# Gated linear attention and a mixture of experts in one kernel: ScalarE issues the small loads, VectorE's two scans run a step ahead, and the routing groups end at other tiles

## The chip, the cores and the metric

The kernel runs on one core of a Trainium2 chip. A core has five engines, each with its own instruction stream that it works off in order: TensorE (PE in the profile; its weight loads are shown apart as PEld), VectorE (DVE), ScalarE (ACT), GpSimd (POOL) and SyncE (SP). They meet through semaphores. Transfers between HBM and the on-chip memory run on 16 DMA engines; an instruction on SP, ACT or POOL starts one. The metric is the device time of one execution in microseconds.

## What is computed

First an attention with a decaying state, for 4 batches, 8 heads, 768 positions and a head size of 48; then a top-1 mixture of 8 experts over the 3072 rows that come out.

```python
for t in range(S):
    state = alpha[:, :, t, :, None] * state + np.einsum('bhd,bhe->bhde', k[:, :, t], v[:, :, t])
    y[:, :, t] = np.einsum('bhd,bhde->bhe', q[:, :, t], state)
...
logits = x @ w_gate + modality_bias[modality_id]
e_idx = np.argmax(logits, axis=1)
...
for e in range(E):
    mask = e_idx == e
    h = np.maximum(x[mask] @ w1[e], 0.0)
    out[mask] = gate_w[mask, None] * (h @ w2[e])
```

The gate weight `gate_w` is the softmax probability of the chosen expert. `x` has 384 columns, an expert's hidden layer 1024.

## The kernel before, in words

**Attention.** The 3072 rows are 24 tiles of 128, six to a batch. A loop over steps s = 0 to 23 is written as a pipeline: step s starts tile s and finishes earlier ones. `decay_in(s)` turns alpha on PE (L249) and copies it to a buffer X (on ACT, L258; two X buffers). `decay` (L263) and `decay_back` (L274) are two scans on DVE that make the running products of alpha, G and F. `scale(s-1)` turns k and q on PE and multiplies them with G and F on DVE (`kh` L290, `qh` L293). `rows(s-3)` turns a finished tile back (L369) and stores it to a DRAM buffer `xd`. `natural(s-1)` turns `kh` back (L299), `state`, `scores` and `outputs` (L331, L311, L338) are the products of the attention, `update` (L356) carries the state on. `logits` and `logits_rows` (L381, L389, L391) give the expert logits of two tiles at a time. `guard` (L278, ACT) looks for values of alpha out of range. The turned tiles share a ring of three PSUM buffers called `tr`; `scores` and the small products of the routing share a ring of two called `sc`.

**Loads.** `load` (L133) issues on SP one DMA for each of alpha, k, q and v of a tile: 1024 pieces of 192 bytes. A ring of four buffers holds each of alpha, k and q, six hold v; tile names end in the buffer, so `nat_a2` is alpha of tiles 2, 6, 10 and so on. SP also loads the gate weights `wgp` in four small DMAs at step 1 (L155), the modality numbers `mi` and biases `mbb` at step 2 (L161, L162), and stores `xd` (L374).

**Routing.** `GROUPS` lists (after, t0, t1): once the logits of tile `after` are there, tiles t0 to t1 - 1 are routed by a flow of small DVE and PE instructions which is cut into pieces. `advance()` runs the next piece of each open flow, twice in a step. The pieces of a group are A (L449 to L454), B (L457 to L464) and C (L467 to L477). For the two group ends named in `EARLY`, further pieces pick the fullest expert: D (L539 to L546) counts, E (L548 to L564) finds its rows and starts the load of its weights, F (L571, L527 to L532) makes their indices, G gathers them. So the experts' part can start before the routing of all tiles is known. Behind the loop, the last pieces are written out by hand among the last attention products and the first hidden units of the first early expert (`first_unit`, L124). `route_end` (L591) turns the counts into the table of the remaining work.

**Experts.** Long stretches of matmuls (L1007 to L1009, L1026 to L1028), each factor split into a rounded part and a rest. Weights come by SP (L665, L667), rows and gates by POOL (L693, L699).

**Order and semaphores.** PE, DVE and ACT run in the order of the program text; SP's and POOL's order comes from a scheduler when the program is built. The builder gives the DMAs that SP and ACT issue eight completion semaphores, DMAHW0 to DMAHW7, in turn by its own schedule. An instruction that issues a DMA waits until the earlier DMA on the same semaphore has landed.

Of the kernel before, what the change touches and what calls it, by code (L numbers as in the profile page):

```python
# [41 lines left out]
U = T // P  # L42
NG = 2 * E

EARLY = (16, 18)
NA = len(EARLY)
NE = NA * TE // T
SU = N // T
# [7 lines left out]
AMIN = 1.0e-17  # L56
AFLOOR = 1.0e-30

GROUPS = ((5, 0, 6), (11, 6, 12), (15, 12, 16), (17, 16, 18), (21, 18, 22), (23, 22, 24))


@with_exitstack
def attention_moe(ctx: ExitStack, tc: tile.TileContext, q, k, v, alpha, mid, wg, mb, w1, w2, out):
# [81 lines left out]

    warm(7)
    wgp = ac.tile([P, 2, 2, 32], F32, name="wgp")
    pool.memset(wgp, 0.0)
    mi = ac.tile([NU, P, 2], I32, name="mi")
    mbb = ac.tile([P, NM, E], F32, name="mbb")  # L150

    def load_gate():
        for c in range(2):
            for g in range(2):
                sp.dma_start(  # L155
                    wgp[64 * c : 64 * c + D, g, :, :E],
                    wg.rearrange("(h c g d) e -> c g d h e", c=2, g=2, d=D)[c, g],
                )

    def load_modality():  # L160
        sp.dma_start(mi.rearrange("t p w -> t (p w)"), mid.bitcast(I32).rearrange("(t x) -> t x", t=NU))  # L161
        sp.dma_start(mbb, mb.unsqueeze(0).broadcast_to([P, NM, E]))  # L162


    DR = na.tile([P, SEGS], F32, name="DR")[:, : NP * SEG + 1]
    vec.memset(DR, 0.0)
    vec.memset(DR[:, SEG :: SEG], 1.0)
# [53 lines left out]
    def bias_table():  # L221
        mf = ac.tile([NU, P], F32, name="mf")
        vec.tensor_copy(mf, mi[:, :, 0])
        yield
        mp = ps.tile([P, NU], F32, name="kv")
        pe.transpose(mp, mf, ident[:NU, :NU])
        mt = ac.tile([P, NU], F32, name="mt")
        vec.tensor_copy(mt, mp)
        tmp = ac.tile([P, NU, E], F32, name="btt")
        for m in range(NM):  # L230
            sel = ac.tile([P, NU], F32, name=f"msel{m}")
            vec.tensor_scalar(sel, mt, float(m), None, op0=ALU.is_equal)
            vec.tensor_tensor(
                tmp if m else bt,
                sel.unsqueeze(2).broadcast_to([P, NU, E]),
                mbb[:, m].unsqueeze(1).broadcast_to([P, NU, E]),
                op=ALU.mult,
            )
            if m:
                vec.tensor_tensor(bt, bt, tmp, op=ALU.add)  # L240


    def seg(t, lo):
        return t.rearrange("p (a b) -> p a b", b=SEG)[:, :, lo : lo + P]

    def trans(i, n):
        p = ps.tile([P, NP, P], F32, name="tr", bufs=3)
        for j in range(NP):
            pe.transpose(  # L249
                p[:, j], nat[n, i % NB][:, 2 * j : 2 * j + 2].rearrange("p a b -> p (a b)"), ident  # L250
            )
        if i < 2 or (i == 2 and n == "a"):
            warm(1)
        return p

    def decay_in(i):
        pa = trans(i, "a")
        (act.copy if i else vec.tensor_copy)(seg(X[i % 2][:, 1:], 0), pa)  # L258
# [18 lines left out]
    def guard(i):  # L277
        act.activation(  # L278
            junk.rearrange("p (a b) -> p a b", b=D),
            nat["a", i % NB][:, :, :D].bitcast(U32),  # L280
            AF.Relu,
            bias=bhi,
            scale=1.0,
            accum_out=gacc[:, i : i + 1],
        )

    def scale(i):
        kh = sb.tile([P, NP, P], F32, name="kh")
        pk = trans(i, "k")
        vec.tensor_tensor(kh, pk, seg(st[i, "G"][:, 1:], 1), op=ALU.mult)  # L290
        qh = sb.tile([P, NP, P], F32, name="qh", bufs=3)
        pq = trans(i, "q")
        vec.tensor_tensor(qh, pq, seg(st[i, "F"], 1), op=ALU.mult)  # L293
        st[i, "k"], st[i, "q"] = kh, qh

    def natural(i):
        p = ps.tile([P, NP, P], F32, name="tr", bufs=3)
# [133 lines left out]
    def route_begin():  # L431
        vec.memset(ohs, 0.0)
# [5 lines left out]
    def route_flow(t0, t1):  # L438
        n = t1 - t0
        s = slice(t0, t1)  # L440
        sh = [P, n, E]

        def wide(a, m=E):
            return a[:, s].unsqueeze(2).broadcast_to([P, n, m])

        def over(a, m=E):
            return a.unsqueeze(1).broadcast_to([P, n, m])

        vec.tensor_tensor(L[:, s], L[:, s], bt[:, s], op=ALU.add)  # L449
        vec.tensor_reduce(mx[:, s], L[:, s], axis=AX.X, op=ALU.max)  # L450
        vec.tensor_tensor(ls[:, s], L[:, s], wide(mx), op=ALU.subtract)
        vec.scalar_tensor_tensor(eq[:, s], ls[:, s], 0.0, over(rev), op0=ALU.is_equal, op1=ALU.mult)
        vec.tensor_reduce(m2[:, s], eq[:, s], axis=AX.X, op=ALU.max)
        vec.tensor_tensor(oh[:, s], eq[:, s], wide(m2), op=ALU.is_equal)  # L454
        yield
        rp = ps.tile([P, n, E], F32, name="sc", bufs=2)
        pe.matmul(rp, tri, oh[:, s], start=True, stop=False)  # L457
        for t in range(t0, t1 - 1):
            m = t1 - 1 - t
            pe.matmul(  # L460
                rp[:, t + 1 - t0 :], ones, oh[:, t].unsqueeze(1).broadcast_to([P, m, E]), start=False, stop=False
            )
        pe.matmul(rp, ones, ohs.unsqueeze(1).broadcast_to(sh), start=False, stop=True)
        vec.tensor_tensor(rk[:, s], rp, oh[:, s], op=ALU.mult)  # L464
        yield
        with nc.allow_low_precision("whole numbers"):
            vec.tensor_reduce(r1[:, s], rk[:, s], axis=AX.X, op=ALU.add)  # L467
        if t1 == NU and n > 2:
            vec.tensor_reduce(hsum, oh[:, t0 : t1 - 1].rearrange("p t e -> p e t"), axis=AX.X, op=ALU.add)
            vec.tensor_tensor(ohs, ohs, hsum, op=ALU.add)  # L470
        elif t1 < NU:
            vec.tensor_reduce(hsum, oh[:, s].rearrange("p t e -> p e t"), axis=AX.X, op=ALU.add)
            vec.tensor_tensor(ohs, ohs, hsum, op=ALU.add)
        vec.tensor_scalar(hr[:, s], r1[:, s], 7, None, op0=ALU.arith_shift_right)
        vec.tensor_scalar(lo[:, s], r1[:, s], P - 1, None, op0=ALU.bitwise_and)
        vec.scalar_tensor_tensor(hi[:, s], m2[:, s], -float(NU), hr[:, s], op0=ALU.mult, op1=ALU.add)
        vec.tensor_tensor(OL[:, s], over(ioh, P), wide(lo, P), op=ALU.is_equal)  # L477
# [113 lines left out]
    def route_end(na):  # L591
# [3 lines left out]
        cnt = ps.tile([P, E], F32, name="kv")  # L595
        pe.matmul(cnt, ones, ohs, start=True, stop=False)
        pe.matmul(cnt, ones, left, start=False, stop=False)
        if na:
            pe.matmul(cnt, ones, oh[:, NU - 2], start=False, stop=False)
        pe.matmul(cnt, ones, oh[:, NU - 1], start=False, stop=True)  # L600
        vec.tensor_tensor(
            nj.rearrange("p e u j -> p e (u j)"),
            cnt.unsqueeze(2).broadcast_to([P, E, 2 * NJ]),
# [239 lines left out]
    def split2(w, j):  # L843
        return split("w2", WR[w][1][:, 2 * j : 2 * j + 2])

    route_begin()
    mctx = ExitStack()
    manual = {mybir.EngineType.PE, mybir.EngineType.DVE, mybir.EngineType.Activation}
    mctx.enter_context(tc.manual_schedule(engines=manual))
    for s in range(NU):  # L850
        if s > 0 and s + PF < NU:
            load(s + PF, "a")
        if s > 0 and s + PF - 1 < NU:
            load(s + PF - 1, "kqv")
        if s == 1:
            load_gate()
        if s == 2:
            load_modality()
        if s == 4:
            sp.dma_start(xd[MID : MID + 1], zr)  # L860
            sp.dma_start(gd[MID : MID + 1], zr[:, 0:1])
        if s != 1:
            decay_in(s)
        if live(s - 1):
            scale(s - 1)
        if s == 1:
            decay_in(s)
        if live(s - 3):
            rows(s - 3)
        if live(s - 4) and s % 2:  # L870
            logits_rows(s - 4)
        advance()
        if live(s - 1) and (s - 1) % NC < NC - 1:
            natural(s - 1)
        decay(s)
        if s < NU - 1:
            advance()
        if s % 2:
            groups(s - 4)
        decay_back(s)  # L880
        guard(s)
        if s == 5:
            start(bias_table())
            half_index()
        if live(s - 3) and (s - 3) % 2:
            logits(s - 3)
        if live(s - 2):
            state(s - 2)
        if live(s - 1):
            scores(s - 1)  # L890
        if live(s - 2):
            outputs(s - 2)
        if live(s - 1):
            update(s - 1)
# [7 lines left out]
    hpool["h"] = rctx.enter_context(tc.tile_pool(name="hp", bufs=8, side="right"))  # L902
    w2s, hs = {0: []}, {0: []}

    advance()
    early = flows.pop()
    logits(L0 - 2)
    state(L0 - 1)
    scores(L0)
    outputs(L0 - 1)  # L910
    logits_rows(L0 - 2)
    group = route_flow(GROUPS[-1][1] - 4, GROUPS[-1][1])
    next(group)
    next(early)
    state(L0)
    rows(L0 - 1)
    next(group)
    outputs(L0)
    for _ in group:
        pass  # L920
    next(early)
    first_inputs()
    logits(L0)
    rows(L0)
    logits_rows(L0)
    last = route_flow(GROUPS[-1][1], NU)
    next(last)
    flag = out_of_range()
    next(flag)
    first_unit(0)  # L930
    next(last)
    ends = route_end(NE)
    next(ends)
    first_unit(1)
    next(early)
    first_unit(2)
    next(ends)
# [315 lines left out]
```

## Time and profile before

| | us |
|---|---|
| median of 3 runs | 374.81 |
| lowest and highest | 373.77 and 374.91 |
| the profiled execution, own time | 375.57 |
| its span, first to last instruction | 373.6 |
| mean granted PE clock | 0.989 |
| DVE, ACT, POOL busy | 224.8, 189.0, 151.6 |

In the profile, times count from the start of the span. A row of the timeline has the start, the length, the engine, the line, the operation and the tiles (out<-in), how many instructions it merges, and in brackets the idle time before it and what ended it. "SPq" marks an instruction of SP's that issues a DMA; its length is the time that SP spent on it, not the transfer. The attention loop runs to about 141 us, its end and the routing to 164 us, the experts from there.

### The profile page before, as it was taken

Reading aid. Unit: us, or ns where it says so; the run is one execution under the profiler, and the core shown is the slowest. Engines: PE = TensorE matmul, PEld = TensorE weight load, DVE = VectorE, ACT = ScalarE, POOL = GpSimd, SP = SyncE. Lnnn points to the kernel's source line nnn. Section 1 sums busy time; section 2 is a strip of 40 time slices with the busy share of each in tenths; the row PEclk is TensorE's granted clock in tenths of the full one; section 3 lists DMA queues with packets and bytes.
Section 4 is the critical chain, followed back from the end, with each engine's and each line's share of the span. In section 5 each row is a group of like instructions: output and inputs, shape, how many; then the busy total and the mean of one; then the engine's idle time right before and its main releaser. Section 6 shows DMA issues by size and latency. Waiting matters only on the chain. (4 is left out here: it accounts for less than half of the span.)

```text
span 373.6 us, 9370 instructions
## 1 busy us (share of the span) xinstructions
PE 359.1 (96%) x3666; PEld 317.0 (85%) x3666; DVE 224.8 (60%) x455; ACT 189.0 (51%) x367; POOL 151.6 (41%) x218
## 2 busy tenths in 40 slices
PE   7998999999999899999999999999999999999992
PEld 4787788889888788799998898899889988978992
DVE  6886979878979977895746506531661455036400
ACT  2666677677678464446554425433551454154310
POOL 9945244534444345283146335412722372220021
PEclk9999999999999989999999999999999999999997
DMA  9989999999999994849756416431723374110011
GB/s 139 165 123 159 208 192 194 183 185 190 198 183 186 194 380 160 294 171 359 223 157 204 155 44 227 154 107 48 270 84 120 131 214 145 45 44 5 1 45 49
DMA packets 122846, 59.18 MB, mean 158 GB/s; under 512 B 102977, under 2 KB 114296, under 8 KB 122792
## 3 DMA queue, kind: packets, MB, share of 16 engines
q1 hardware_dynamic: 118824, 48.83, 58.5%
q0 software_dynamic: 3968, 9.65, 7.7%
q8 instruction: 31, 0.51, 0.6%
q14 instruction: 23, 0.19, 0.2%
HBM read 49.01 MB, written 9.50 MB: 157 GB/s over the span
## 5 line engine op out<-in xcount | busy, mean ns | idle before, releaser
L973 POOL DMA_INDIRECT out_dram<-os,odx x23 | 23.1, 1004 | 110.0 <-ACT os L1041 93.3
L1007 PE MATMUL sc<-w2H,hH 128*128 128x384 f32 x192 | 65.0, 338 | 0.0
L316 POOL TENSOR_SCALAR_AFFINE_SELECT scT<-scT 128x512 f32<-128x512 f32 x48 | 38.4, 822 | 65.3 <-ACT scT L315 65.3
L1009 PE MATMUL sc<-w2H,hL 128*128 128x384 f32 x192 | 64.2, 334 | 0.0
L1008 PE MATMUL sc<-w2L,hH 128*128 128x384 f32 x192 | 64.2, 334 | 0.0
L837 DVE TENSOR_TENSOR w1L<-w1r,w1H 128x768 fp32r<-128x768 f32 x24 | 22.0, 955 | 67.6 <-ACT w1H L835 67.6
L1026 PE MATMUL tr<-xH,w1H 128*128 128x512 f32 (+1 forms) x144 | 53.8, 374 | 0.0
L1028 PE MATMUL tr<-xH,w1L 128*128 128x512 f32 (+1 forms) x144 | 53.5, 372 | 0.0
L1027 PE MATMUL tr<-xL,w1H 128*128 128x512 f32 (+1 forms) x144 | 53.5, 371 | 0.0
L829 DVE SCALAR_TENSOR_TENSOR hL<-tr,hH 128x512 fp32r<-128x512 f32 x47 | 32.4, 689 | 31.5 <-ACT hH L827 31.3
L827 ACT ACTIVATE hH<-tr 128x512 fp32r<-128x512 f32 x47 | 28.1, 598 | 45.5 <-PE tr L1028 42.0
L1041 ACT ACTIVATE os<-sc,gg 128x384 f32<-128x384 f32 x23 | 13.4, 582 | 67.4 <-PE sc L1009 43.5
L1007 PEld LDWEIGHTS sc<-w2H,hH 128*128 128x128 f32 x192 | 36.1, 188 | 1.1 <-issue 1.0
L1008 PEld LDWEIGHTS sc<-w2L,hH 128*128 128x128 f32 x192 | 36.1, 188 | 0.0
L1009 PEld LDWEIGHTS sc<-w2H,hL 128*128 128x128 f32 x192 | 36.0, 188 | 0.0
L699 POOL DMA_INDIRECT gg<-gd,idx x25 | 26.6, 1063 | 21.9 <-DMA gd<-gs 14.9
L315 ACT COPY scT<-sc 128x512 f32<-128x512 f32 x48 | 25.8, 589 | 12.6 <-PE sc L311 12.6
L693 POOL DMA_INDIRECT xg<-xd,idx x25 | 27.0, 1081 | 11.7 <-issue 4.9
L274 DVE TENSOR_TENSOR_SCAN Fw<-X,DF 128x516 f32<-128x516 f32 x24 | 31.0, 1291 | 0.8
L1028 PEld LDWEIGHTS tr<-xH,w1L 128*128 128x128 f32 x144 | 27.1, 188 | 4.7
L1026 PEld LDWEIGHTS tr<-xH,w1H 128*128 128x128 f32 x144 | 27.1, 188 | 4.6
L1027 PEld LDWEIGHTS tr<-xL,w1H 128*128 128x128 f32 x144 | 27.1, 188 | 4.6
(245 smaller groups left out, 684.2 us busy)
## 6 DMA issues: line engine op xcount, KB each, us to landing
w1r<-in_moe_w_dram SPq DMA_DIRECT2D x16, 768.0 KB, 4.8
w2r<-in_moe_w_dram SPq DMA_DIRECT2D x16, 768.0 KB, 4.5
nat_a<-in_alpha_dram SPq DMA_DIRECT2D x24, 192.0 KB, 3.7
nat_k<-in_k_dram SPq DMA_DIRECT2D x24, 192.0 KB, 5.5
nat_q<-in_q_dram SPq DMA_DIRECT2D x24, 192.0 KB, 4.8
vt<-in_v_dram SPq DMA_DIRECT2D x24, 192.0 KB, 4.6
xd<-xs SPq DMA_DIRECT2D x24, 192.0 KB, 4.9
xg<-xd,idx POOLq DMA_INDIRECT x25, 5.4
```

Of the source, the lines that this page charges most:

```text
L274: vec.tensor_tensor_scan(Fw, x[:, :-1], d, 0.0, op0=ALU.mult, op1=ALU.add)
L316: pool.affine_select(s, s, [[0, NP], [1, P]], ALU.is_ge, 0.0, base=0, channel_multiplier=-1)
L693: pool.indirect_dma_start(xg[x][:, u], None, xd[0:rows], IOA(idx[:, c : c + 1], 0), bounds_check=rows - 1, oob_is_err=False)
L699: pool.indirect_dma_start(gg[x][:, u : u + 1], None, gd[0:rows], IOA(idx[:, c : c + 1], 0), bounds_check=rows - 1, oob_is_err=False)
L827: act.activation(hH, hp, AF.Relu)
L829: vec.scalar_tensor_tensor(hL, hp, 0.0, hH.bitcast(F32), op0=ALU.max, op1=ALU.subtract)
L1007: pe.matmul(op, hH[:, us] if f is None else hH[:, f, us], wH, start=first, stop=False)
L1008: pe.matmul(op, hH[:, us] if f is None else hH[:, f, us], wL, start=False, stop=False)
L1009: pe.matmul(op, hL[:, us] if f is None else hL[:, f, us], wH, start=False, stop=final)
L1026: pe.matmul(hp, wH[:, d, fs], XH[:, d, :n], start=(d == 0), stop=False)
L1027: pe.matmul(hp, wH[:, d, fs], XL[:, d, :n], start=False, stop=False)
L1028: pe.matmul(hp, wL[:, d, fs], XH[:, d, :n], start=False, stop=(d == ND - 1))
```

## The change

ScalarE issues the six small loads: the four of `wgp` before the loop, `mi` and `mbb` at the start of step 3. The clearing of `wgp` moves from POOL to DVE. From step 8 on, `decay_in`, `decay` and `guard` run for the tile after the current one; from step 12 on `decay_back` too (at steps 8 and 12 both tiles are done). At step 0 `kh` is made right behind the first scan. The groups end at 6, 12, 16, 20 and 24 tiles instead of 6, 12, 16, 18, 22 and 24, and the early choices stand after 16 and 20 tiles, not 16 and 18. Three short dummy matmuls (`warm`) fall away. The bias table uses a `sc` buffer instead of `kv` and is cut into more pieces.

```diff
-EARLY = (16, 18)
+EARLY = (16, 20)
...
-GROUPS = ((5, 0, 6), (11, 6, 12), (15, 12, 16), (17, 16, 18), (21, 18, 22), (23, 22, 24))
+GROUPS = ((5, 0, 6), (11, 6, 12), (15, 12, 16), (19, 16, 20), (23, 20, 24))
+T0 = GROUPS[-1][1]
+LEAD = (8, 12)
...
-    pool.memset(wgp, 0.0)
+    vec.memset(wgp, 0.0)
...
-    def load_gate():
-        for c in range(2):
-            for g in range(2):
-                sp.dma_start(
...
-    def load_modality():
-        sp.dma_start(mi.rearrange("t p w -> t (p w)"), mid.bitcast(I32).rearrange("(t x) -> t x", t=NU))
-        sp.dma_start(mbb, mb.unsqueeze(0).broadcast_to([P, NM, E]))
...
+    for c in range(2):
+        for g in range(2):
+            act.dma_start(
+                wgp[64 * c : 64 * c + D, g, :, :E],
...
-        mp = ps.tile([P, NU], F32, name="kv")
+        mp = ps.tile([P, NU], F32, name="sc", bufs=2)
...
-        if i < 2 or (i == 2 and n == "a"):
+        if i == 0 or (i == 1 and n == "a"):
             warm(1)
...
+    def lead(s, w):
+        return [i for i in ((s, s + 1) if s == LEAD[w] else (s + (s > LEAD[w]),)) if i < NU]
...
-        if s == 1:
-            load_gate()
-        if s == 2:
-            load_modality()
...
+        if s == 3:
+            act.dma_start(mi.rearrange("t p w -> t (p w)"), mid.bitcast(I32).rearrange("(t x) -> t x", t=NU))
+            act.dma_start(mbb, mb.unsqueeze(0).broadcast_to([P, NM, E]))
+        ins = lead(s, 0)
         if s != 1:
-            decay_in(s)
+            decay_in(ins[0]) if ins else None
...
-        decay(s)
+        steps = [(decay, i) for i in lead(s, 0)] + [(decay_back, i) for i in lead(s, 1)]
+        steps.sort(key=lambda x: x[1])
+        for f, i in steps[:1]:
+            f(i)
+        if s == 0:
+            scale_keys(s)
         if s < NU - 1:
             advance()
         if s % 2:
             groups(s - 4)
-        decay_back(s)
-        guard(s)
+        for f, i in steps[1:]:
+            f(i)
+        for i in ins:
+            guard(i)
...
-    advance()
-    early = flows.pop()
+    (early,) = flows
+    next(early)
     logits(L0 - 2)
+    next(early)
     state(L0 - 1)
     scores(L0)
+    next(early)
     outputs(L0 - 1)
     logits_rows(L0 - 2)
-    group = route_flow(GROUPS[-1][1] - 4, GROUPS[-1][1])
-    next(group)
     next(early)
...
     first_unit(0)
+    first_unit(1)
     next(last)
     ends = route_end(NE)
     next(ends)
-    first_unit(1)
     next(early)
```

The next rows are ACT's in the changed kernel from the end of step 2 into step 3; before, the row of S is followed by that of X. S belongs to the state, X to alpha of tile 3, and the brackets name the semaphores waited for.

```order
L347 COPY yt<-y 128x512 [waits PE_49]
L359 COPY S<-kv 128x192 [waits PE_49]
L862 DMA mi<-in_moe_modality_id_dram 24x256 [waits DMAHW0_49]
L863 DMA mbb<-in_moe_modality_bias_dram 128x16 [waits DMAHW1_49]
L254 COPY X_165<-tr 128x4x128 [waits DVE_49,PE_49]
L374 COPY xs<-tr 128x2x4x48 [waits PE_49]
```

The two small loads stand ahead of the copies of step 3, and each waits for a DMA semaphore. SP's rows in the changed kernel, from v of tile 3 on, show who else uses these two semaphores (in brackets the semaphore of each DMA; buffers k0, q0 hold tile 4, a1 tile 5, a2 tile 6, k2 and q2 tile 6; vt4 and vt5 are v of tiles 4 and 5).

```order
L135 DMA vt3_109<-in_v_dram 128x8x48 [waits DMAHW4_49]
L135 DMA nat_a1_85<-in_alpha_dram 128x8x48 [waits DMAHW5_49,PE_49,Activation_49]
L135 DMA nat_k0_81<-in_k_dram 128x8x48 [waits DMAHW6_49]
L135 DMA nat_q0_83<-in_q_dram 128x8x48 [waits DMAHW7_49]
L135 DMA vt4_111<-in_v_dram 128x8x48 [waits DMAHW0_49]
L135 DMA vt5_113<-in_v_dram 128x8x48 [waits DMAHW1_49]
L859 DMA xd_60<-zr_188 1x384 [waits DMAHW2_49,Pool_49]
L860 DMA gd_61<-zr_188 1x1 [waits DMAHW3_49]
L135 DMA nat_k1_87<-in_k_dram 128x8x48 [waits DMAHW4_49,PE_49]
L135 DMA nat_q1_89<-in_q_dram 128x8x48 [waits DMAHW5_49,PE_49]
L135 DMA nat_a2_91<-in_alpha_dram 128x8x48 [waits DMAHW6_49,Activation_49]
L135 DMA vt0_103<-in_v_dram 128x8x48 [waits DMAHW7_49,PE_49]
```

The DMA after these on SP (`nat_k2`) takes DMAHW2: numbers 0 and 1 are those of `mi` and `mbb`. So the wait of `mi` is for four landings on DMAHW0 (alpha of tile 0, the fourth `wgp`, v of tile 2, v of tile 4), that of `mbb` for four on DMAHW1 (k of tile 0, alpha of tiles 2 and 4, v of tile 5). Before, the four loads of `wgp` stood between vt3 and nat_a1, and `mi` and `mbb` between vt4 and vt5.

DVE's rows from the last of piece E at step 21 to `kh` of step 22, first before the change, then with it.

```order
L564 TENSOR_TENSOR OHE<-OHE,tok_207 128x32
L449 TENSOR_TENSOR L<-L,bt 128x16
L450 TENSOR_REDUCE mx<-L 128x2
L451 TENSOR_TENSOR ls<-L,mx 128x16
L452 SCALAR_TENSOR_TENSOR eq<-ls,rev 128x16
L453 TENSOR_REDUCE m_213<-eq 128x2
L454 TENSOR_TENSOR oh<-eq,m_213 128x16
L271 TENSOR_SCALAR amin<-G 128x4
L272 RECIPROCAL DF_163<-amin 128x4
L274 SCALAR_TENSOR_TENSOR Fw<-X_161,DF_163 128x516
L290 TENSOR_TENSOR kh<-tr,G 128x512
```

```order
L565 TENSOR_TENSOR OHE<-OHE,tok_211 128x32
L267 TENSOR_SCALAR amin<-G 128x4
L268 RECIPROCAL DF_163<-amin 128x4
L270 SCALAR_TENSOR_TENSOR Fw<-X_161,DF_163 128x516
L286 TENSOR_TENSOR kh<-tr,G 128x512
```

Piece A of the group that ended at 18 is gone from this place. PE's rows behind the loop in the changed kernel, from the last scores on; before, the two counts (L539, L541) stood in step 23, ahead of the scores of tile 22.

```order
L312 MATMUL sc<-qh,kh 64x128 x16
L540 LDWEIGHTS ones
L540 MATMUL sc<-ohs,ones 128x8
L542 LDWEIGHTS ones
L542 MATMUL sc<-left,ones 128x8
L339 MATMUL y<-scT,vt_111 64x128 x8
L390 MATMUL kv<-ident,lts 128x128 x2
L332 MATMUL y<-qh,T_173 64x128 x8
L370 MATMUL tr<-ident,yt 128x128 x4
L572 LDWEIGHTS OL
L572 MATMUL sc<-OHE,OL 128x2
```

Piece D of the second early choice has moved behind the last scores, and piece F (L572) behind `state` and `rows`.

More of the change, by code (lines that the diff above doesn't have):

```diff
@@ L147, in attention_moe @@
     wgp = ac.tile([P, 2, 2, 32], F32, name="wgp")
-    pool.memset(wgp, 0.0)
+    vec.memset(wgp, 0.0)
     mi = ac.tile([NU, P, 2], I32, name="mi")
     mbb = ac.tile([P, NM, E], F32, name="mbb")
-    def load_gate():
-        for c in range(2):
-            for g in range(2):
[L155 to L158, printed above, removed]
-    def load_modality():
-        sp.dma_start(mi.rearrange("t p w -> t (p w)"), mid.bitcast(I32).rearrange("(t x) -> t x", t=NU))
-        sp.dma_start(mbb, mb.unsqueeze(0).broadcast_to([P, NM, E]))
+    for c in range(2):
+        for g in range(2):
+            act.dma_start(
+                wgp[64 * c : 64 * c + D, g, :, :E],
+                wg.rearrange("(h c g d) e -> c g d h e", c=2, g=2, d=D)[c, g],
+            )
     DR = na.tile([P, SEGS], F32, name="DR")[:, : NP * SEG + 1]
@@ L230, in bias_table @@
         for m in range(NM):
+            yield
             sel = ac.tile([P, NU], F32, name=f"msel{m}")
@@ L285, in guard, with scale_keys @@
         )
-    def scale(i):
+    def scale_keys(i):
         kh = sb.tile([P, NP, P], F32, name="kh")
@@ L290, in scale @@
         vec.tensor_tensor(kh, pk, seg(st[i, "G"][:, 1:], 1), op=ALU.mult)
+        st[i, "k"] = kh
+    def scale(i):
+        if i:
+            scale_keys(i)
         qh = sb.tile([P, NP, P], F32, name="qh", bufs=3)
@@ L293, in scale @@
         vec.tensor_tensor(qh, pq, seg(st[i, "F"], 1), op=ALU.mult)
-        st[i, "k"], st[i, "q"] = kh, qh
+        st[i, "q"] = qh
     def natural(i):
@@ L467, in route_flow @@
             vec.tensor_reduce(r1[:, s], rk[:, s], axis=AX.X, op=ALU.add)
-        if t1 == NU and n > 2:
+        if t1 == NU and t0 < T0:
             vec.tensor_reduce(hsum, oh[:, t0 : t1 - 1].rearrange("p t e -> p e t"), axis=AX.X, op=ALU.add)
@@ L597, in route_end @@
         pe.matmul(cnt, ones, left, start=False, stop=False)
-        if na:
-            pe.matmul(cnt, ones, oh[:, NU - 2], start=False, stop=False)
-        pe.matmul(cnt, ones, oh[:, NU - 1], start=False, stop=True)
+        for t in range(T0 if na else NU - 1, NU):
+            pe.matmul(cnt, ones, oh[:, t], start=False, stop=(t == NU - 1))
         vec.tensor_tensor(
@@ L861, in attention_moe @@
             sp.dma_start(gd[MID : MID + 1], zr[:, 0:1])
+        if s == 3:
+            act.dma_start(mi.rearrange("t p w -> t (p w)"), mid.bitcast(I32).rearrange("(t x) -> t x", t=NU))
+            act.dma_start(mbb, mb.unsqueeze(0).broadcast_to([P, NM, E]))
+        ins = lead(s, 0)
         if s != 1:
-            decay_in(s)
+            decay_in(ins[0]) if ins else None
         if live(s - 1):
             scale(s - 1)
-        if s == 1:
-            decay_in(s)
+        for i in ins[s != 1 :]:
+            decay_in(i)
         if live(s - 3):
@@ L916, in attention_moe @@
     rows(L0 - 1)
-    next(group)
+    next(early)
     outputs(L0)
-    for _ in group:
-        pass
-    next(early)
     first_inputs()
@@ L924, in attention_moe @@
     rows(L0)
+    next(early)
     logits_rows(L0)
-    last = route_flow(GROUPS[-1][1], NU)
+    last = route_flow(T0, NU)
     next(last)
```

## The prediction

> **What bounds the kernel now.** I read the page's busy times first, then its slices for PE.
>
> ```profile
> PE 359.1 (96%) x3666; PEld 317.0 (85%) x3666; DVE 224.8 (60%) x455; ACT 189.0 (51%) x367; POOL 151.6 (41%) x218
> PE   7998999999999899999999999999999999999992
> ```
>
> PE is busy all along, so the kernel is as long as PE's work and its few holes: span 373.6 less 359.1 busy leaves 14.5 us, some at both ends. A change that takes no work from PE (this one takes three short dummies) can only close holes or open new ones. The timeline of PE by step shows three of them.
>
> ```profile
> 36.24 0.66 PE L249 MATMUL tr<-ident,nat_a 128*128 128x128 f32 x4 [1.78 <-DMA nat_a<-in_alpha_dram]
> 38.81 0.64 PE L381 MATMUL kv<-yt,wgp 128*32 128x256 f32 x8 [0.41 <-DVE mt L228]
> 129.84 0.87 PE L299 MATMUL tr<-ident,kh 128*128 128x128 f32 x4 [1.63 <-DVE kh L290]
> ```
>
> A window of 4 us shows what follows the third.
>
> ```profile
> 130.00:134.00 4.00, 4.00 (x60) 2.71 (x59) 3.79 (x20) 1.45 (x4) 2.24 (x2) 0.57 1.03 388
> ```
>
> In a window's row the third number from the end is the granted clock. In the 4 us behind the 1.63 us hole it is 0.57: 4 x 0.43 = 1.7 us of PE's work lost. That hole costs 3.3 us, not 1.6.
>
> **The first hole: the loads are late.** The order of SP's DMAs and PE's wait say why.
>
> ```profile
> 18.89 1.12 SPq L133 DMA_DIRECT2D vt<-in_v_dram  x1
> 20.11 3.58 SPq L155 DMA_DIRECT2D wgp<-in_moe_w_gate_dram  x4
> ...
> 24.85 0.73 SPq L133 DMA_DIRECT2D nat_q<-in_q_dram  x1
> ...
> 26.41 1.37 SPq L161 DMA_DIRECT2D mi<-in_moe_modality_id_dram  x1
> 27.82 0.36 SPq L162 DMA_DIRECT2D mbb<-n_moe_modality_bias_dram  x1
> 28.23 0.43 SPq L133 DMA_DIRECT2D vt<-in_v_dram  x1
> ...
> 31.27 1.07 SPq L133 DMA_DIRECT2D nat_a<-in_alpha_dram  x1
> ```
>
> ```profile
> 20.00:22.00 2.00, 2.00 (x59) 1.83 (x60) 1.90 (x4) 1.60 (x4) 0.04 (x1) 1.00 1.14 172
> 22.00:24.00 2.00, 2.00 (x36) 1.95 (x33) 0.81 (x1) 1.80 (x5) 1.75 (x3) 1.00 0.18 16
> ```
>
> While SP issues the four `wgp` loads the traffic falls from 172 to 16 GB/s, and alpha of tile 6, issued at 31.27, comes 1.78 us late. Without the six small loads SP has 3.58 + 1.37 + 0.36 = 5.3 us more ahead of it, so this hole closes: **-1.8 us**. The Trainium skill, "DMA: Bandwidth & Descriptors", section "Issuing engines are not separate DMA queues", says that DMAs from several engines share the same 16 DMA engines and that a second issuer saves only the sequencer's time, usually little. By it the hole would stay and the sum below be 1.8 us higher. The 16 GB/s row speaks against that here: the sequencer's time was what the stream lacked.
>
> The second hole is the bias table's `kv` buffer; it gets a `sc` buffer and later pieces: **-0.4 us**. The third comes from DVE, where piece A of the group 16 to 18 stands ahead of the second scan and so of `kh`.
>
> ```profile
> 125.71 0.65 DVE L449 TENSOR_TENSOR L<-L,bt 128x16 f32<-128x16 f32 x1
> 127.56 0.16 DVE L271 TENSOR_SCALAR amin<-G 128x4 f32<-128x4 f32 x1
> ```
>
> A takes 127.56 - 125.71 = 1.85 us there, more than the hole, and the change has none at this place. The hole and its slow clock go: **-3.3 us**.
>
> **What the change adds: a wait on ACT.** The load of `mi` waits for the fourth landing on DMAHW0. SP's and ACT's rows give the four: alpha of tile 0, the last `wgp`, v of tile 2, v of tile 4. The load of `mbb` waits in the same way for v of tile 5, the 22nd load of the stream. ACT works in order, so behind these two stand the copy of X for tile 3 and all that ACT does later. The timeline of ACT and PE shows when ACT gets there.
>
> ```profile
> 17.62 0.33 ACT L358 COPY S<-kv 128x192 f32<-128x192 f32 x1
> 18.17 0.59 ACT L258 COPY X<-tr 128x512 f32<-128x512 f32 x1 [0.22 <-PE tr L249]
> 18.84 0.62 PE L369 MATMUL tr<-ident,yt 128*128 128x128 f32 x4
> ```
>
> ACT is there at about 18 us, when SP is still issuing v of tile 3 (18.89). PE's L369 needs the `tr` buffer that X's copy frees, and DVE's scan of tile 3 needs X, so PE and DVE stop too. When does v of tile 5 land?
>
> ```profile
> 4.81 1.07 SPq L133 DMA_DIRECT2D nat_a<-in_alpha_dram  x1
> ...
> L133 SPq DMA_DIRECT2D vt<-in_v_dram x5: 428/1090/1142, 8.4 to 28.2; - x5
> ```
>
> The view of line L133 in that stretch also has their time to land.
>
> ```profile
> DMA to landing us min/median/max: 4.6/5.0/5.4
> ```
>
> From alpha of tile 2 at 4.81 to v of tile 3 at 18.89 lie 11 loads, (18.89 - 4.81) / 11 = 1.28 us each, and the loads of v from 8.4 to 28.2 us land 5.0 us after issue (4.6 to 5.4). The next five (alpha 5, k 4, q 4, v 4, v 5) go on at that pace: v of tile 5 is issued at 18.89 + 5 x 1.28 = 25.3 and lands at 30.3. `mi` is issued before that, `mbb` takes 0.36, so X's copy starts at about 30.7 and not at 18.17: **+12.5 us**. None of these five loads waits for ACT's or PE's later work, so nothing hides the wait and nothing prolongs it.
>
> Bounds: if the pace rose to the 0.73 us of q's load right behind `wgp` (24.85), and the landing took 4.6 us, X's copy would start at 18.89 + 5 x 0.73 + 4.6 + 0.4 = 27.5, +9.3; if v of tile 5 came no sooner than before (28.23 + 4.6 = 32.8) and the issue took the 1.37 us of `mi`, at 34.2, +16.0.
>
> **The clock after that stop.** The trace has two nearest cases. The 1.63 us hole cost 1.7 us. The start gives the other end: PE works from 1.26 us on, and a dummy product takes 0.63 us still at 6.36 and 0.38 at 7.46.
>
> ```profile
> 1.26 3.17 PE L144 MATMUL y<-still 128*128 128x512 bf16 x7 [1.26 <-DVE still L139]
> 6.36 0.63 PE L144 MATMUL y<-still 128*128 128x512 bf16 x1
> 7.46 0.38 PE L144 MATMUL y<-still 128*128 128x512 bf16 x1
> ```
>
> That is some 6 us at half speed, 3.1 us lost. A stop of 12 us is nearer to the start than to the hole: **+2.5 us** (1.7 to 3.1). The Trainium skill, "TensorE: Matmul & The Clock Gate", section "What's actually happening", has a gate that halves the clock after an idle window of about 3.4 us and opens it after a busy one; by it the loss is half of 3.4 to 6.8 us, the same range. The length of the slow stretch here agrees; that a hole of 1.63 us was enough does not.
>
> **The other parts.** Behind the loop PE gets three new waits. The rows of before that price them:
>
> ```profile
> 144.78 1.07 ACT L315 COPY scT<-sc 128x512 f32<-128x512 f32 x2 [1.14 <-PE sc L311]
> ...
> 143.01 0.15 DVE L548 TENSOR_REDUCE base<-rest 128x1 f32<-128x8 f32 x1
> 144.75 0.20 DVE L564 TENSOR_TENSOR OHE<-OHE,tok 128x36 f16<-128x36 f16 x1
> 153.61 0.17 DVE L464 TENSOR_TENSOR rk<-sc,oh 128x16 f32<-128x16 f32 x1
> 155.67 0.27 DVE L617 SCALAR_TENSOR_TENSOR diag<-ident,kc,dz 128x52 bf16<-128x52 f32 x1
> ```
>
> Piece D's count now stands right behind the last scores and shares their two buffers, so it waits for the first of ACT's two copies: half of 1.07 and the way there, some 0.8 us. F needs E's chain, 144.75 + 0.20 - 143.01 = 1.94 us, with `state` and `rows` (about 1 us) to cover it: 1.1 us with the hops. The table's first product needs 155.67 + 0.27 - 153.61 = 2.3 us of DVE with one hidden unit (1.4 us) ahead of it where two stood: 0.8 us. The sum is 2.7; about 0.7 us of small holes that PE has at these places now goes: **+2.0 us** (0 if DVE, which does no scan in step 23, is ahead by that much; 3 if none of the holes goes). The second expert's weights are asked for some 3 us later, but are used only at about 165 us, with 8 us between their landing and that now.
>
> The scans a step ahead put a scan of 1.2 us more into step 8 and both scans into step 12; DVE's steps have 1.5 us of slack beside PE's 5.5. **+0.5 us** (0 to 1.5). The earlier `kh` of step 0 and the dummies change only what comes before ACT's stop, which ends at a time that the loads set: nothing.
>
> **The sum**, against the profiled execution's own 375.57 us: -1.8 - 0.4 - 3.3 + 12.5 + 2.5 + 2.0 + 0.5 = +12.0, 387.6 us. The median of the runs lies 0.76 us below that execution, so **386.8 us**, 3.2% slower.
>
> **Rivals.**
>
> *ACT does not stop.* Then the useful parts are left: 374.81 - 5.5 + 2.0 + 0.5 = **371.8 us**, faster. It needs v of tile 5 to have landed when ACT gets there at 18 us, or the DMA to be queued without holding ACT. Against the first: 21 loads take 21 x 1.28 us at the trace's pace; the wait vanishes only from a pace under 0.6 us per load. Against the second: the table of SP's waits shows an issuer that stands at a wait, up to 6.9 us for ACT.
>
> ```profile
> SPq L374 <- ACT xs L373: 9.6, 4, 6.9
> ```
>
> Chance 0.10.
>
> *It does not stop, and the earlier alpha is late.* From step 8 on alpha is turned one step sooner. Before, alpha of tile 9 was issued here:
>
> ```profile
> 47.47 0.37 SPq L133 DMA_DIRECT2D nat_a<-in_alpha_dram  x1
> 47.57 0.66 PE L249 MATMUL tr<-ident,nat_a 128*128 128x128 f32 x4
> ```
>
> The page's list of DMA issues has the landing of alpha, from issue, in its last column.
>
> ```profile
> nat_a<-in_alpha_dram SPq DMA_DIRECT2D x24, 192.0 KB, 3.7
> ```
>
> With 3.7 us to land that is 51.2, and step 8 would want it at about 49: up to 2.2 us back, 374.0 us, no change. With ACT's stop the loads get far ahead and this is nothing. Chance 0.04.
>
> *ACT stops and more is lost.* The new holes behind the loop, 2.7 us within some 10, bring the clock to half once more, as the 1.63 us did: +1.7, 388.5 us. It lies within the range. Chance 0.15.
>
> **How the numbers follow.** ACT's stop has 0.86 in all, of which 0.71 for the sum and 0.15 with a second slow stretch. The bounds of its terms added at one end give 374.81 + 9.3 + 1.7 - 5.5 = 380.3 and at the other 374.81 + 16.0 + 3.1 - 5.5 + 3 + 1.5 = 392.9; 381 to 392 holds nearly all of the 0.86, say 0.8. A measurement of this kernel can tell about 0.3% (1.1 us) from no change. Faster than that: 0.10; within it: 0.04; slower: 0.86.
>
> **What would show it.** In the timeline of the changed kernel ACT's row of X for tile 3 would stand at about 31 us with an idle time of some 13 us ended by a DMA of v or by `mi`/`mbb`, PE's slices near the tenth of the span would be empty, and the granted clock behind them 0.5. PE's waits for alpha (1.8 us) and for `kh` (1.6 us) would be gone, and PE would wait at the count, at the product of OHE and OL and at the table's product behind the loop. If X's copy still starts near 18 us, the forecast is wrong and the first rival holds.

## The result: 3.5% slower

The changed kernel takes 388.46 us (median of 4 runs, 387.38 to 388.98), the kernel before 374.86 us (four runs now). The ratio is 1.035 (95% interval 1.030 to 1.040). The profiled execution of the changed kernel took 388.75 us, its span is 386.7 us, 13.1 us more than before's 373.6.

The page of the changed kernel, first PE's busy time, then its slices and the granted clock in the same 40 slices of 9.7 us:

```profile
PE 359.7 (93%) x3666; PEld 318.0 (82%) x3666; DVE 223.4 (58%) x442; ACT 189.3 (49%) x367; POOL 152.7 (39%) x217
...
PE   7807999999999999889999999999999999999992
...
PEclk9975999999999999999999999999999999999999
```

PE has the same work (359.7 against 359.1 us). Its third slice is empty and the fourth runs at about half clock: that is where the time went. The timeline of ACT, from the end of step 2 on, names the instructions:

```profile
17.48 0.33 ACT L359 COPY S<-kv 128x192 f32<-128x192 f32 x1
29.05 0.56 ACTq L862 DMA_DIRECT2D mi<-in_moe_modality_id_dram  x1
30.25 0.36 ACTq L863 DMA_DIRECT2D mbb<-n_moe_modality_bias_dram  x1
30.71 0.58 ACT L254 COPY X<-tr 128x512 f32<-128x512 f32 x1 [12.90 <-DMA vt<-in_v_dram]
```

ACT is done with S at 17.8 us and issues `mi` only at 29.05. SP's rows say what it waited for: the two loads of v of tiles 4 and 5, issued from 23.76 on in 2.31 us.

```profile
23.76 2.31 SPq L135 DMA_DIRECT2D vt<-in_v_dram  x2
```

The three loads just ahead of them (issued from 20.21 on) land 5.2 to 5.3 us after issue, so v of tile 4 is there at about 29.0, the time of `mi`, and v of tile 5, issued at 24.93, at about 30.1, the time of `mbb`. The copy of X, which could have run at about 18.0, starts at 30.71. PE, in its own timeline, stops with it:

```profile
18.26 0.60 PE L245 MATMUL tr<-ident,nat_q 128*128 128x128 f32 x4
31.35 1.11 PE L370 MATMUL tr<-ident,yt 128*128 128x128 f32 x4 [12.49 <-ACT X L254]
```

The windows of the same stretch show the clock (third number from the end):

```profile
18.90:23.30 4.40, 0.00 (x0) 0.00 (x0) 0.85 (x2) 0.00 (x0) 0.85 (x2) 1.00 1.07 174
23.40:31.30 7.90, 0.00 (x0) 0.00 (x0) 0.00 (x0) 0.58 (x1) 0.00 (x0) 0.50 1.38 164
31.40:37.00 5.60, 5.60 (x66) 4.94 (x68) 2.74 (x4) 2.48 (x6) 0.15 (x1) 0.50 1.24 187
37.00:41.00 4.00, 4.00 (x57) 3.20 (x53) 1.92 (x3) 2.63 (x6) 2.18 (x4) 1.00 0.54 104
```

The clock falls to half 4.5 us into the stop and stays there for the first 5.7 us in which PE works again: 2.8 us of work lost. The DMA engines move 164 to 174 GB/s all through the stop. The loads did not stop, only the compute engines did.

The table of PE's waits for the rest of the attention and the routing (total us, times, longest):

```profile
PE tr L300 <- DVE kh L286: 1.6, 3, 0.6
...
PE sc L540 <- ACT scT L316: 0.7, 1, 0.7
PE kv L682 <- DVE nj L601: 0.5, 1, 0.5
PE y L332 <- ACT yt L347: 0.5, 1, 0.5
PE kv L622 <- DVE diag L617: 0.4, 1, 0.4
PE tr L245 <- DMA nat_a<-in_alpha_dram: 0.4, 1, 0.4
PE kv L623 <- DVE diag L619: 0.2, 1, 0.2
```

The wait of 1.78 us for alpha of tile 6 is gone, and of that of 1.63 us for `kh` of tile 21 there is 0.58 us left (at 142.83, one of the three in the first row). The rows from L540 on, without the one for alpha, are new waits behind the loop.

### The profile page after: what moved, and what is told of

It is laid out like the page before. It is cut to its first block, busy times and chain, and to the rows that moved or that the text cites. A ratio compares the mean times of both kernels' runs of the same rounds, so it can differ in the third digit from the quotient of the medians.

```text
span 386.7 us, 9342 instructions
## 1 busy us (share of the span) xinstructions
PE 359.7 (93%) x3666; PEld 318.0 (82%) x3666; DVE 223.4 (58%) x442; ACT 189.3 (49%) x367; POOL 152.7 (39%) x217
## 5 line engine op out<-in xcount | busy, mean ns | idle before, releaser
L981 POOL DMA_INDIRECT out_dram<-os,odx x23 | 23.9, 1039 | 108.7 <-ACT os L1049 92.9
L259 DVE TENSOR_TENSOR_SCAN G<-X,DR 128x516 f32<-128x516 f32 x24 | 30.4, 1268 | 11.6 <-ACT X L254 11.6
L316 ACT COPY scT<-sc 128x512 f32<-128x512 f32 x48 | 25.8, 589 | 13.9 <-PE sc L312 13.9
```

Of the source, the lines that this page charges most:

```text
L259: vec.tensor_tensor_scan(G[:, 1:][:, ::-1], x[:, 1:][:, ::-1], DR[:, 1:][:, ::-1], 0.0, op0=ALU.mult, op1=ALU.add)
```

## The experiments

**e1: the two loads at step 1.** Theory: ACT's stop is a wait for landings that stand far ahead in the stream. Rivals: the two DMAs cost this time wherever ACT issues them, or something of step 3 does it. At step 1 the same two DMAs wait only for early `wgp` landings.

```diff
-        if s == 3:
+        if s == 1:
             act.dma_start(mi...)
             act.dma_start(mbb...)
```

> The changed kernel with the loads of mi and mbb issued by ACT at step 1, not 3. There each of the two waits for one landing of a small load of wgp (DMAHW2 and DMAHW4), which the changed kernel's trace has at 5.6 to 8 us, before ACT gets there at about 6.5 us or little later. Theory (the stop is the wait for landings far ahead in the stream of loads): no stop of more than 1.5 us, the stop of 12.5 us and the slow clock of 2.8 us behind it go, 388.5 - 15.3 = 373.2 us (372.2 to 374.5). Rival (the issue of these two DMAs on ACT among its copies, or their traffic, costs the time wherever it stands): 385 us or more.

Measured: 377.84 us, ratio to before 1.010 (1.007 to 1.014), span 375.8 us. ACT's copy of X of tile 3 starts at 18.03 us:

```profile
17.49 0.33 ACT L359 COPY S<-kv 128x192 f32<-128x192 f32 x1
18.03 0.59 ACT L254 COPY X<-tr 128x512 f32<-128x512 f32 x1 [0.22 <-PE tr L245]
```

The stop is gone, so its cause is the wait and not the DMAs. But 373.2 us was expected, and 4.6 us are missing. The timeline of PE and that of SP show where they are:

```profile
45.87 0.60 PE L245 MATMUL tr<-ident,nat_q 128*128 128x128 f32 x4
49.77 1.09 PE L245 MATMUL tr<-ident,nat_a 128*128 128x128 f32 x4 [3.30 <-DMA nat_a<-in_alpha_dram]
```

```profile
46.12 0.39 SPq L135 DMA_DIRECT2D nat_a<-in_alpha_dram  x1
```

```profile
49.20:52.50 3.30, 2.73 (x13) 2.43 (x13) 1.86 (x2) 1.06 (x2) 0.00 (x0) 0.50 1.29 194
```

At step 8, the first with the scans ahead, PE wants alpha of tile 9 at 46.5 us. SP issues its load at 46.12 and it lands at 49.63. The window behind it has half clock, 1.4 us lost. Together 4.7 us. In the changed kernel this hole does not show, because the stop let the loads run ahead: there alpha of tile 9 lands at 50.94 and is used at 61.49.

**e2: the two loads at step 2.** There they wait for the landings of q of tile 3 and alpha of tile 5.

```diff
-        if s == 3:
+        if s == 2:
```

> The changed kernel with the two loads on ACT at step 2. Now mi waits for the third landing on DMAHW3, that of q of tile 3, and mbb for the third on DMAHW5, that of alpha of tile 5, which the changed kernel's trace has at 20.21 + 5.22 = 25.4 us. Theory: ACT is there at 13.0 us and makes its copy of X of tile 2 at about 25.8, a stop of 12.8 us, one step earlier than in the changed kernel and ended by an alpha load, not a v load; half clock behind it for 3.4 to 6.8 us of work; 387 to 390 us. Rival (what stops ACT is something of step 3 alone, such as the buffers that X of tile 3 and v of tile 5 use): 373 us, no stop.

Measured: 388.13 us, ratio 1.037 (1.032 to 1.042). ACT's timeline:

```profile
12.37 0.34 ACT L359 COPY S<-kv 128x192 f32<-128x192 f32 x1
23.13 0.56 ACTq L862 DMA_DIRECT2D mi<-in_moe_modality_id_dram  x1
25.54 0.36 ACTq L863 DMA_DIRECT2D mbb<-n_moe_modality_bias_dram  x1
25.99 0.58 ACT L254 COPY X<-tr 128x512 f32<-128x512 f32 x1 [13.29 <-DMA mi<-in_moe_modality_id_dram]
```

X of tile 2 is copied at 25.99 (25.8 expected). The stop goes with the landings that the two DMAs wait for, one step earlier and at another copy; the rival of step 3 alone falls.

**e3: the two loads at step 3, issued by POOL,** whose DMAs do not use the eight semaphores.

```diff
         if s == 3:
-            act.dma_start(mi...)
-            act.dma_start(mbb...)
+            pool.dma_start(mi...)
+            pool.dma_start(mbb...)
```

> The changed kernel with the two loads at the same place, step 3, issued by POOL, whose DMAs don't use these eight semaphores. Theory: no wait, ACT's copy of X of tile 3 at about 18 us, 373.2 us (372.2 to 375, since POOL may be late with its own work by 1 to 2 us). Rival (the traffic of the two loads at that time, or a late mi, stops the pipeline): 385 us or more.

Measured: 379.05 us, ratio 1.013 (1.007 to 1.019). X of tile 3 is copied at 18.49: no stop at the same place in the program. POOL issued the two loads already at 5.38 and 6.13 us, so e3 takes them out of ACT's order but does not try their traffic at the time of step 3. As in e1, PE waits for alpha of tile 9 (3.4 us), which the expectation left out.

**e4: the kernel before, with `mi` and `mbb` alone moved to ACT at step 3.**

```diff
-        if s == 2:
-            load_modality()
+        if s == 3:
+            act.dma_start(mi...)
+            act.dma_start(mbb...)
```

> The kernel before with one edit: mi and mbb are issued by ACT at the start of step 3 and not by SP in step 2; wgp stays on SP. The two wait for the fourth landing on DMAHW0 and DMAHW1, here of v of tiles 4 and 5. v of tile 5 was issued at 28.23 with 1.7 us of the two loads ahead of it on SP, so at 26.5 now, and lands at 31.5. Theory: ACT, there at 17.9 us, copies X of tile 3 at about 31.9; stop +13.7, slow clock +2.8, the wait for alpha of tile 6 gone -1.8: +14.7, 389.5 us (387 to 392). Rival (the loss belongs to the other parts of the change together, such as the scans ahead or the wgp loads on ACT): within 2 us of 374.9.

Measured: 386.92 us, ratio 1.037 (1.032 to 1.043), just below the range expected. ACT's timeline:

```profile
30.86 0.37 ACTq L859 DMA_DIRECT2D mbb<-n_moe_modality_bias_dram  x1
31.33 0.58 ACT L258 COPY X<-tr 128x512 f32<-128x512 f32 x1 [13.39 <-DMA vt<-in_v_dram]
```

The copy starts at 31.33 (31.9 expected), and this one edit makes as much of a loss as the whole change. The rest of the change is then worth about nothing beside the stop. Of the 2.6 us that are missing to the 389.5 expected, 1.6 are the slow clock behind the wait for `kh` of tile 21, which this execution does not have: from the k turn of tile 21 to that of tile 22 it takes 8.19 us, before 9.74. e5 to e8 take the rest apart without the stop.

**e5: e1 without the scans ahead.**

```diff
-LEAD = (8, 12)
+LEAD = (NU, NU)
```

> The kernel of e1 (loads of mi and mbb at step 1) without the scans a step ahead (LEAD after the last step). What is open: e1 has no stop and is still 1% above before, and its trace has one new hole, PE waiting 3.30 us for alpha of tile 9 at step 8, with half clock behind it (some 1.2 us), and 0.8 us ahead of kh at step 13. Theory A (these belong to the scans ahead, which want alpha of tile 9 one step sooner than the stream of loads brings it): both go, 5.3 us less than e1, 0.4 to 0.6% below before, about 372.5 us where before is 374 to 375. Theory B (the loads on ACT or the new groups make the late alpha): the wait for alpha stays, within 1 us of e1 (377.8).

Measured: 376.76 us, where the kernel before took 377.41 us beside it, ratio 0.998 (0.995 to 1.001). Against e1's 1.010 that is 1.2%, 4.6 us: the wait for alpha of tile 9 is gone and so is the slow clock behind it. The scans ahead cause both (theory A). It is no clear gain over before, though; 0.4 to 0.6% was expected.

**e6: e5 with the groups, and the work behind the loop, of before.** It is before with `wgp` on ACT and cleared by DVE, `mi` and `mbb` on ACT at step 1, the bias table in `sc`, and the early `kh` and dummies of the change.

```diff
-EARLY = (16, 20)
+EARLY = (16, 18)
...
-GROUPS = ((5, 0, 6), (11, 6, 12), (15, 12, 16), (19, 16, 20), (23, 20, 24))
+GROUPS = ((5, 0, 6), (11, 6, 12), (15, 12, 16), (17, 16, 18), (21, 18, 22), (23, 22, 24))
```

> As e5, with the routing groups and the work behind the loop of the kernel before. It tells what the new groups alone are worth: e5 less e6. By the traces of before and of the changed kernel the hole ahead of kh at step 21 comes back with its slow clock (+2.7 us against the changed kernel's 0.6 us there), and the stretch from the last step to the first product of the experts is 2.6 us shorter. Theory: within 1 us of e5, both 372 to 373.5 us. Rivals: the groups are a gain (e6 slower than e5 by over 1.5 us), or a loss (e6 faster by over 1.5 us).

Measured: 374.27 us, ratio 0.992 (0.990 to 0.995), 2.5 us less than e5. "Within 1 us" fell: the new groups are a loss. They save most of the hole at `kh` of tile 21 and lose more behind the loop. From the k turn of the last tile to the experts' first product e5 takes 163.66 - 136.99 = 26.67 us, e6 162.79 - 138.37 = 24.42 us. Two rows of e5's timeline of PE, one of the new waits behind the loop and one in the experts:

```profile
141.42 0.17 PE L540 MATMUL sc<-ohs,ones 128*128 128x8 bf16 x1 [0.74 <-ACT scT L316]
...
166.57 0.44 PE L1016 MATMUL sc<-w2L,hH 128*128 128x384 f32 x1 [1.45 <-DVE w2L L837]
```

The first is the groups': the count stands behind the scores. The second is not: e1, e8 and the changed kernel have the same groups and no such wait. At the hole (a wait of 1.64 us in e6, 0.59 in e5), from the k turn of tile 21 to that of tile 22, e5 takes 131.89 - 123.96 = 7.93 us and e6 133.25 - 123.50 = 9.75 us with its slow clock. So in these two traces the groups lose 2.25 us and save 1.82. Without a slow clock they save less: e10, which is e6 once more on another chip, has none and takes 8.19 us there and 23.38 us behind the loop, and beside it e5 loses 3.0 us. The 2.5 us between the medians lie between these two readings, with the wait for w2L in them; what the groups alone cost stays open.

**e7: e6 with the scans ahead from steps 17 and 18,** where alpha lands some 5 us ahead of its use.

```diff
-LEAD = (NU, NU)
+LEAD = (17, 18)
```

> As e6, with the scans ahead from steps 17 and 18 on. In before's trace alpha of tile 9 lands 2.0 us ahead of its use and that of tiles 17 to 22 some 5.4 us. Theory: at step 17 the earlier alpha is there, and the scans, a step ahead, are done by step 21, so that piece A of the group ending at 18 no longer makes kh late: the hole of 1.6 us and its slow clock of 1.7 us go, and 0 to 0.8 us come for the two steps with a scan more; 2.5 us less than e6, about 370 us. Rivals: alpha is late at step 17 too (a wait of 1 us or more for alpha there, no gain); or kh is late at step 21 as before, since kh stands behind piece A in DVE's order whatever the scans do.

Measured: 376.85 us, ratio 0.999 (0.996 to 1.001), 2.6 us slower than e6 instead of 2.5 us faster. PE's timeline:

```profile
110.25 0.66 PE L312 MATMUL tr<-ident,kh 128*128 128x128 f32 x4 [1.11 <-DVE kh L298]
116.08 0.66 PE L312 MATMUL tr<-ident,kh 128*128 128x128 f32 x4 [0.19 <-DVE kh L298]
129.41 0.65 PE L312 MATMUL tr<-ident,kh 128*128 128x128 f32 x4 [1.63 <-DVE kh L298]
```

Alpha is in time, as the theory had it. But the hole is there as in e6 (1.63 us in the last row, 1.64 in e6), and the steps with a scan more add two waits, 1.3 us together, ahead of it. So a scan made earlier does not help a `kh` that stands behind piece A in DVE's order.

**e8: e5 with the scans ahead from steps 17 and 18.**

```diff
-LEAD = (NU, NU)
+LEAD = (17, 18)
```

> As e5, with the scans ahead from steps 17 and 18 on. With these groups no piece A stands at step 21, so the scans ahead have little to hide: 0.6 us of the wait for kh at step 21 can go and 0 to 0.8 us come at steps 17 and 18. Theory: within 1 us of e5. Rival: e7's gain comes from the scans ahead by themselves, and shows here too (2 us less than e5).

Measured: 376.18 us, ratio 0.999 (0.996 to 1.002), within 1 us of e5: the scans ahead gain nothing here either.

**e9 and e10: `kh` of tile 21 ahead of piece A.** e6 with one `kh` moved, beside e6 itself on one chip.

```diff
-        if i:
+        if i not in (0, 21):
             scale_keys(i)
...
-        if s == 0:
+        if s in (0, 21):
             scale_keys(s)
```

> As e6, and kh of tile 21 is made right behind the first scan of step 21, ahead of the early choice's pieces and of piece A on DVE, as the change does at step 0. In e6's trace DVE is busy without a break from 108.64 to 132.3 us and makes this kh at 126.38, behind piece A (122.97 to 124.9) and the second scan (125.23 to 126.4); PE waits 1.64 us for it and then has half clock for 3.4 us. Theory (the order on DVE makes the hole, not the scans' lateness): PE's wait for kh at step 22 goes; qh, which is still behind the second scan, makes PE wait 0.4 to 0.9 us ahead of the scores; 0.8 to 1.2 us less than e6, and up to 1.7 us more where the slow clock no longer follows: ratio to before 0.985 to 0.990. Rival (DVE's whole load in steps 19 to 22 is the bound, in whatever order): the wait for qh takes all of the 1.6 us, within 0.5 us of e6.

> e6 once more, beside e9 on the same chip. Its ratio to before was 0.9923 (0.9897 to 0.9948). 0.990 to 0.995 expected.

Measured: e9 371.07 us, ratio 0.991 (0.988 to 0.995); e10 372.34 us, ratio 0.994 (0.990 to 0.997). The timeline of PE in e9 at step 22:

```profile
125.91 0.64 PE L312 MATMUL tr<-ident,kh 128*128 128x128 f32 x4
126.48 0.64 PE L394 MATMUL kv<-yt,wgp 128*32 128x256 f32 x8
127.05 0.67 PE L344 MATMUL y<-qh,T 64*64 64x128 f32 x16
128.31 0.43 PE L324 MATMUL sc<-qh,kh 48*64 48x128 f32 x2 [0.59 <-DVE vals L541]
129.05 1.10 PE L324 MATMUL sc<-qh,kh 48*64 48x128 f32 x30 [0.32 <-DVE rk L477]
```

The wait for `kh` is gone, and 0.9 us of waiting comes back at the scores: for the `sc` buffers that pieces F and B give back through DVE (`vals`, `rk`), not for qh as expected. In these two traces, both at full clock there, the move gains next to nothing: from the turn of alpha of tile 21 to that of tile 23 e9 takes 131.56 - 117.86 = 13.70 us, e10 131.30 - 117.53 = 13.77 us. That fits the rival, by which DVE's whole load is the bound in whatever order, though PE now waits at `sc` and not for qh.

In the median e9 is 1.3 us faster than e10; the two intervals overlap, and its ratio is just above the 0.985 to 0.990 expected. The granted clock of the runs suggests where the 1.3 us come from: all twelve of e9 have 0.993 or more, seven of e10's twelve 0.992 or less. The five others of e10 have a median of 371.21 us, next to e9's 371.07. So the move seems to pay by the slow clock that no longer follows, and not by the wait itself. Both kernels beat the one before and the changed one: e9 is 0.9% below before where the change is 3.5% above.

## Why the prediction was right, step by step

The forecast was 386.8 us, in a range of 381 to 392, by a stop of ACT; 388.46 was measured. The terms, from the trace of the changed kernel against before's (a step lasts from its first turn of alpha on PE to the next step's first turn):

| term | predicted | measured | from |
|---|---|---|---|
| ACT's stop | +12.5 | +12.5 | PE's idle time at 31.35 |
| slow clock behind it | +2.5 | +2.8 | half of 5.7 us |
| hole at alpha of tile 6 | -1.8 | -1.9 | step 5: 7.38 to 5.52 |
| hole at the bias table | -0.4 | -0.5 | step 6: 5.63 to 5.15 |
| hole at `kh`, with its slow clock | -3.3 | -2.7 | step 22: 9.74 to 7.05 |
| scans ahead | +0.5 | +0.9 | step 13: 5.53 to 6.38 |
| behind the loop | +2.0 | +2.6 | below |
| sum | +12.0 | +13.7 | |

The last of them is the stretch from the k turn of the last tile to the experts' first product, 164.50 - 141.11 = 23.4 us before. The same two rows of the changed kernel, from PE's timeline:

```profile
152.00 0.66 PE L245 MATMUL tr<-ident,nat_k 128*128 128x128 f32 x4
...
177.98 0.42 PE L1015 MATMUL sc<-w2H,hH 128*128 128x384 f32 x1
```

That is 26.0 us. The spans differ by 13.1; the rest is 0.1 us less up to step 3 and 0.4 us less in the experts.

- **The place and length of the stop** were right: the copy of X was forecast for 30.7 and came at 30.71. That it fits to the hundredth is luck: SP came to v of tile 3 at 19.43 and not at 18.89, needed (24.93 - 19.43) / 5 = 1.10 us and not 1.28 for each of the next five loads, and the landing took some 5.3 us instead of 5.0; the three errors cancel. e2 and e4 put the landing elsewhere and the stop followed it (25.99 and 31.33); e1 and e3 took the wait away and the stop was gone.
- **The clock** lay between the two cases that bounded it. The rule that the prediction took from the Trainium skill, "TensorE: Matmul & The Clock Gate", section "What's actually happening", gave an estimate of half of 3.4 to 6.8 us. Half of 5.7 was measured.
- **The first hole** closed as forecast, in the changed kernel and in e1, where no stop hides it: the small loads on ACT gave SP time back. In e1 alpha of tile 6 is issued at 28.91 us, before at 31.27: 2.4 us sooner, which is enough for the hole, but less than half of the 5.3 us that the prediction counted, as SP now spends 1.0 to 1.3 us on each of the loads from 20.57 to 25.38 (before, 0.73 on that of q right behind `wgp`). The prediction had set beside it the Trainium skill, "DMA: Bandwidth & Descriptors", section "Issuing engines are not separate DMA queues", by which a second issuer usually saves little and the hole would stay. For this stream the trace does not agree.
- **Four terms were too small or too good by 1.9 us in all**: the slow clock (0.3), the `kh` hole, of which 0.6 us stays (0.6), the scans ahead (0.4), and the work behind the loop (0.6). The two other holes gave 0.1 us more each than forecast, so the sum is 1.7 us too low, which is the whole difference to the measured time. The work behind the loop has the three places that the prediction named: the count L540 waits 0.74 us (0.8 forecast), the table's products 0.48 + 0.44 + 0.24 = 1.2 us (0.8), OHE and OL (L572) no wait that the table shows (1.1; in e5 it is 0.17), and a fourth, `yt` ahead of L332 with 0.46, that it did not name. So the size of this term is in part luck, too.
- **The rival without a stop was priced wrongly.** "The useful parts are left", 371.8 us, is not what the kernel does without the stop: e1 has 377.8. The rival of the late alpha, set apart with a chance of 0.04 and 2.2 us, is what happens whenever ACT does not stop. Its wait is 3.3 us and not 2.2, because step 8 comes sooner once the first holes are closed (alpha wanted at 46.5, not at 49), and the slow clock behind it was left out (1.4 us). Without the stop too the change would have been slower than before.

The useful part, as it turned out, is what e6 keeps: it is 0.8% and, on another chip, 0.6% faster than before. In the trace of e10 step 5, where PE had waited for alpha, has gone from 7.38 to 5.52 us, and step 6, where it had waited for the bias table, from 5.63 to 5.15. The scans ahead (e1 against e5, by their ratios to before) and the new groups (e5 against e6) each take time away. What each edit in e6 is worth alone, the early `kh` and the missing dummies among them, was not tried.

## What to carry to other kernels

Before a DMA is moved to an engine that also computes, look up which earlier DMA it must wait for, and when that lands: everything behind it in that engine's order waits as well, here 12.5 us for two loads of under 1 us. When work is taken a step ahead, find the load that it wants a step sooner, and read how long ahead of its use that load lands at this place. When a result is late because it stands behind other work in an engine's order, making its inputs earlier changes nothing (e7). Moving the result itself ends that wait, but look at what then comes late instead: here the wait came back at the next buffers that DVE gives back (e9).

## What the runs showed of the hardware

The clock's slow stretches inside the kernels have lengths that are multiples of 3.41 us: 3.41 before (130.13 to 133.54), 13.65 in the changed kernel (23.35 to 37.00), 3.41 in e1 and in e6. And the same hole is not always followed by one. e6 and e10 are the same kernel with the same wait of 1.64 us for `kh`. Windows of e6, then of e10:

```profile
124.20:127.50 3.30, 1.66 (x31) 1.52 (x28) 3.13 (x9) 0.57 (x2) 0.59 (x2) 1.00 0.94 233
127.60:131.00 3.40, 3.40 (x54) 2.47 (x56) 3.23 (x19) 1.46 (x4) 2.25 (x2) 0.50 0.86 221
```

```profile
123.20:126.50 3.30, 2.36 (x35) 2.21 (x35) 3.06 (x10) 1.47 (x4) 1.63 (x3) 1.00 0.92 154
126.60:129.90 3.30, 2.70 (x62) 1.95 (x64) 3.20 (x13) 1.45 (x4) 1.50 (x2) 1.00 0.86 227
```

If the clock is set anew every 3.41 us by what PE did in the stretch before, then in e6 the whole hole fell into one stretch (PE busy for 1.66 of 3.30 us), and in e10 a border divided it (2.36 and 2.70 us). The borders lie elsewhere in each execution. That reading fits these two executions and e7, whose hole (127.78 to 129.41) a border at 128.06 divides and no slow clock follows; it was not tested by itself.

Two holes of before show that PE's busy time alone does not decide. Counted back from 130.13 in stretches of 3.413 us, the hole that ends at 129.84 lies in the stretch from 126.72 to 130.13, PE is busy for 1.78 us of it, and half clock follows. Nearly all of the hole of 1.78 us that ends at 36.24 lies in the stretch from 34.56 to 37.97, PE is busy for 1.73 us of it, and full clock follows. What sets the two apart stays open. The hole of 1.6 us at `kh` thus cost 1.6 us in e7 and e10 and 3.3 us in before and e6.
